# Five-token runs in both halves of the partitions, two load queues, and early attention in a fused linear-attention and GEGLU kernel

## The chip, the cores and the metric

One core of one Trainium2 chip. The metric is the device time of one execution, in microseconds (us), median of several; all executions compared below are in the fast state, except one single look whose state is unknown. Before: 351.67 us (351.45 to 353.07, 3 runs).

## The reference

Linear attention (softmax of q over the features, of k over the tokens), then a gated feed-forward layer on all tokens:

```python
# q, k, v: (8, 8, 576, 64) fp32, randn * 0.1
q_s = softmax(q, axis=-1);  k_s = softmax(k, axis=2)
kv  = np.einsum('bhsd,bhse->bhde', k_s, v)
att = np.einsum('bhsd,bhde->bhse', q_s, kv)
x   = att.transpose(0, 2, 1, 3).reshape(4608, 512)
g   = x @ w_gate                       # (512, 1536)
out = (0.5 * g * (1 + erf(g / sqrt(2))) * (x @ w_val)) @ w_out   # (1536, 512)
```

The softmaxes are written out in the reference (with a subtracted maximum and 1e-9 in the divisor). Since q and k are small, every token of a head gives almost the same row, so an output with permuted rows is only 0.24% off; this matters for reading "correct" in the experiments.

## The kernel before

Block b of the loop is the feed-forward of 512 tokens of batch b; the last block takes the 64 remaining tokens of all eight batches. Attention of the next batch rides between the 12 steps of a block, except in blocks 0 and 1, where it follows the output matmuls. The parts that the argument touches:

```python
# load: partition p holds tokens 4p .. 4p+3 of every head; 64 tokens remain
def load_main(src, nm, b, h0, h1):
    ...
    nc.sync.dma_start(
        out=tiles[key][:, h0:h1, :],                        # 128 partitions
        in_=src[b, h0:h1, 0:MAIN, :].rearrange("h (p n) d -> p h (n d)", n=NM))

def load_rem(src, nm, b):
    t = rmp.tile([64, H, D], f32, name=f"{nm}r", tag="rm")
    nc.sync.dma_start(out=t, in_=src[b, :, MAIN:S, :].rearrange("h p d -> p h d"))
...
# kv of a pair of heads: five matmuls, one per token of the partition (v must be there, cast)
for n in range(NM + 1):
    nc.tensor.matmul(pskv[:, j, :], ek_b[b % 2][:, n, hp * P:(hp + 1) * P],
                     v16_b[b % 2][:, n, 2 * hp:2 * hp + 2, 0:VW], ...)
...
# store of two tokens per partition, 512 KB
nc.sync.dma_start(
    out=out[b * S:b * S + MAIN, :].rearrange("(p n) c -> p n c", n=NM)[:, ns - 1:ns + 1, :],
    in_=yo)
...
for b in range(B + 1):
    ...
    for fi in range(NFI):
        hts.append(ffn_fi(xt, fi))          # 8 matmuls, gelu on ScalarE, product on VectorE
        ...                                 # b >= 2: a unit of the next batch's attention
    ...
    ffn_out(b, hts, 0)                      # 12 matmuls each, evacuation, store
    ...                                     # b <= 1: attention of b + 1 between these
```

The softmax here doesn't subtract the row's maximum and nothing guards it: scores larger than these inputs give would overflow.

## Time and profile before

| | before |
|---|---|
| time | 351.67 us, profiled span 351.8 |
| PE busy | 319.6 us (91%) |
| mean granted PE clock | 0.98 |
| mean DMA rate | 135 GB/s of a span whose first 79 us are full |
| first gate matmul of block 0 / block 1 / block 2 | 26.5 / 70.9 / 111.8 us |
| a block with attention / without | 34.46 / 31.1 us |
| from the last matmul to the end | 4.7 us |

PE is the bound from 111.8 us on; only the first three blocks and the tail have idle PE time. The rows of the profile that show it stand in the prediction below. Two columns need a word: "PEclk" is the clock that PE was granted (it was 0.50 from 66.0 to 70.7 us; the first four gate matmuls of block 0, after 26.5 us of which PE was busy for 7.3, take 1.71 us and later ones 0.86), and "DMA" is the mean over 16 DMA engines.

### The profile page before, as it was taken

The page shows a single profiled execution, that of the slowest core. Times are in us where ns is not written, and L with a number is a line of the kernel's source. Part 1 is how long each engine was busy: PE and PEld are TensorE (multiplying, and loading weights), DVE is VectorE, ACT ScalarE, POOL GpSimd, SP SyncE. Part 2 cuts the span into 40 slices and gives each one's busy share as a digit, 9 for nine tenths or more (in the row PEclk, how much of TensorE's full clock was granted, in tenths as well). Part 3 has the DMA queues.
Part 4 walks back from the last instruction along what each step waited for, and adds up shares of the span by engine and source line. Part 5 has one row for each costly group of instructions (what it writes and reads, how often), then busy time and mean ns, then how long its engine had stood idle before and what let it go on. Part 6 is the DMA issues. An engine that isn't in the chain of part 4 may idle for free.

```text
span 351.8 us, 4287 instructions
## 1 busy us (share of the span) xinstructions
PE 319.6 (91%) x1680; PEld 152.8 (43%) x1680; DVE 179.9 (51%) x283; ACT 135.7 (39%) x184; POOL 42.4 (12%) x36
## 2 busy tenths in 40 slices
PE   0259999499987999999999999999999999999994
PEld 0234445244443544454444444544544444444441
DVE  2582337934386963396339524953494334334331
ACT  3403363043762247424743483248325123203310
POOL 2376620402000200002000200020000000000000
PEclk9999999789996999999999999999999999999999
DMA  7999999893016900296039404940300020011013
GB/s 192 330 388 386 344 278 284 241 269 94 3 60 188 270 6 2 96 276 153 0 117 287 120 2 135 277 112 0 121 1 0 8 113 0 2 60 60 2 30 89
DMA packets 45395, 47.45 MB, mean 135 GB/s; under 512 B 13632, under 2 KB 38208, under 8 KB 45376
## 3 DMA queue, kind: packets, MB, share of 16 engines
q1 hardware_dynamic: 45376, 47.19, 46.3%
q8 instruction: 13, 0.21, 0.3%
q14 instruction: 6, 0.05, 0.1%
HBM read 37.75 MB, written 9.44 MB: 134 GB/s over the span
## 4 chain that ended last, share of the span: by engine, by line
PE 85%; DVE 10%; DMA 2%; issue 1%; SPq 1%; ACT 0%
PE psg L244 27%; PE psv L248 27%; PE psy L262 24%; DVE eq L169 3%; DVE rq L159 2%; PE psx L226 2%; DMA qt<-in_q_dram 2%; PE pst L205 2%; PE pskv L180 2%; DVE xt L229 1%; DVE yo L267 1%; DVE eqt L208 1%; DVE kv_sb L188 1%; PE pstr L214 1%; DVE rrq L163 0%
## 5 line engine op out<-in xcount | busy, mean ns | idle before, releaser
L253 DVE SCALAR_TENSOR_TENSOR ht<-psv,gl 128x512 f16<-128x512 f32 x108 | 74.1, 686 | 92.1 <-PE psv L248 91.5
L251 ACT ACTIVATE gl<-psg 128x512 f32<-128x512 f32 x108 | 64.5, 597 | 144.7 <-PE psg L244 136.1
L244 PE MATMUL psg<-xt,wg_sb 128*128 128x512 f16 x384 | 101.8, 389 | 0.0
L248 PE MATMUL psv<-xt,wv_sb 128*128 128x512 f16 x384 | 99.5, 382 | 0.0
L262 PE MATMUL psy<-wo_sb,ht 128*128 128x512 f16 x432 | 95.0, 379 | 0.0
L248 PEld LDWEIGHTS <-wv_sb 128*128 128x128 f16 x432 | 42.6, 99 | 52.5 <-issue 2.7
L262 PEld LDWEIGHTS <-ht 128*128 128x128 f16 x432 | 41.8, 98 | 49.4
L244 PEld LDWEIGHTS <-wg_sb 128*128 128x128 f16 x432 | 41.6, 99 | 46.0 <-issue 2.8
L267 DVE TENSOR_SCALAR yo<-psy 128x512 f32<-128x512 f32 x36 | 24.8, 690 | 60.7 <-PE psy L262 60.7
L147 POOL CAST v<-vt 128x2048 f16<-128x2048 f32 (+1 forms) x9 | 16.4, 1824 | 179.7 <-DMA vt<-in_v_dram 166.6
L159 DVE TENSOR_REDUCE rq<-eq 128x20 f32<-128x1280 f16 x16 | 23.6, 1476 | 9.6 <-ACT eq L136 9.6
L169 DVE TENSOR_TENSOR eq<-eq,rrq 128x1280 f16<-128x1280 f16 x16 | 25.4, 1590 | 0.2
L205 PE MATMUL pst<-ident,eq 128*128 128x128 f16 x128 | 11.5, 242 | 14.5 <-DVE rck L185 7.8
L180 PE MATMUL pskv<-v,ek 128*128 128x130 f16 x160 | 12.6, 231 | 9.9 <-POOL v L147 9.5
L129 ACT ACTIVATE eq<-qt 128x2048 f16<-128x2048 f32 (+1 forms) x9 | 15.4, 1709 | 6.4 <-DMA qt<-in_q_dram 6.4
L205 PEld LDWEIGHTS <-eq 128*128 128x128 f16 x128 | 9.0, 108 | 19.3 <-DVE eq L169 9.3
L180 PEld LDWEIGHTS <-ek 128*128 128x128 f16 x160 | 11.1, 102 | 13.7 <-ACT ek L129 6.0
L129 ACT ACTIVATE ek<-kt 128x2048 f16<-128x2048 f32 (+1 forms) x9 | 15.5, 1719 | 3.6 <-DMA kt<-in_k_dram 3.5
L238 ACT CAST xtr<-psxr 128x256 f16<-128x256 f32 x8 | 3.0, 372 | 34.9 <-PE psxr L236 34.9
L226 PE MATMUL psx<-eqt,kv_sb 128*128 128x512 f16 x32 | 14.0, 463 | 1.9 <-DVE eqt L208 1.1
L231 ACT CAST xt<-psx 128x512 f16<-128x512 f32 x20 | 11.7, 585 | 9.6 <-PE psx L226 9.6
L248 PE MATMUL psv<-xtr,wv_sb 128*128 128x512 f16 x48 | 12.3, 379 | 0.0
(33 smaller groups left out, 121.1 us busy)
## 6 DMA issues: line engine op xcount, KB each, us to landing
out_dram<-yo SPq DMA_DIRECT2D x16, 512.0 KB, 2.6
kt<-in_k_dram SPq DMA_DIRECT2D x7, 1024.0 KB, 7.9
vt<-in_v_dram SPq DMA_DIRECT2D x7, 1024.0 KB, 10.3
qt<-in_q_dram SPq DMA_DIRECT2D x7, 1024.0 KB, 10.3
wgst<-in_moe_w_gate_dram SPq DMA_DIRECT2D x3, 1024.0 KB, 12.3
wvst<-in_moe_w_val_dram SPq DMA_DIRECT2D x3, 1024.0 KB, 13.6
wost<-in_moe_w_out_dram SPq DMA_DIRECT2D x3, 1024.0 KB, 14.6
kt<-in_k_dram SPq DMA_DIRECT2D x2, 512.0 KB, 5.9
```

The costliest lines, as they stand in the source:

```text
L129: nc.scalar.activation(out=dst[:, 0:NM, h0 * D:h1 * D].rearrange("p n (h d) -> p h n d", d=D), in_=tiles[(nm, b)][:, h0:h1, :].rearrange(" ...
L159: nc.vector.reduce_sum(rq, eq_b[b % 2][:, :, h0 * D:h1 * D].rearrange("p n (h d) -> p n h d", d=D), axis=mybir.AxisListType.X)
L169: nc.vector.tensor_tensor(out=e, in0=e, in1=rr[(b, h0)].unsqueeze(-1).to_broadcast((P, NM + 1, n, D)), op=ALU.mult)
L180: nc.tensor.matmul(pskv[:, j, :], ek_b[b % 2][:, n, hp * P:(hp + 1) * P], v16_b[b % 2][:, n, 2 * hp:2 * hp + 2, 0:VW], start=(n == 0), sto ...
L205: nc.tensor.transpose(pst[:, j, n * P:(n + 1) * P], eq_b[b % 2][:, n, hp * P:(hp + 1) * P], ident)
L226: nc.tensor.matmul(psx, st[(b, "kv", hp)].rearrange("p h e -> p (h e)"), st[(b, "eqt")][:, hp, 0:MAIN], start=True, stop=True)
L244: nc.tensor.matmul(psg, wg_sb[:, ci, fi * P:(fi + 1) * P], xt[:, ci, :], start=(ci == 0), stop=(ci == HP - 1))
L248: nc.tensor.matmul(psv, wv_sb[:, ci, fi * P:(fi + 1) * P], xt[:, ci, :], start=(ci == 0), stop=(ci == HP - 1))
L251: nc.scalar.activation(out=gl, in_=psg, func=ACTF.Gelu)
L253: nc.vector.scalar_tensor_tensor(out=ht, in0=psv, scalar=_H_SCALE, in1=gl, op0=ALU.mult, op1=ALU.mult)
L262: nc.tensor.matmul(psy, hts[fi][:, ns * P:(ns + 1) * P], wo_sb[:, fi, :], start=(fi == 0), stop=(fi == NFI - 1))
L267: nc.vector.tensor_scalar(out=yo[:, ns % 2, :], in0=psy, scalar1=1.0 / _H_SCALE, scalar2=None, op0=ALU.mult)
```

## The change

Its intent is to start PE earlier and close its gaps in blocks 0 and 1. A group of nine tokens now belongs to a pair of partitions m and 64 + m; each of the two loads a run of five (the middle token twice), so the small "remainder" transfers go. Each load and the store pattern are therefore built from two halves of 64 partitions. The start orders q, k, v on two queues, weights come in 1 KB pieces, PE is warmed with idle matmuls, batches 1 and 2 get their attention inside blocks 0 and 1, the last two blocks change places, and the last evacuation (the copy of PE's finished results before a store) is split over two engines.

```diff
-        nc.sync.dma_start(
-            out=tiles[key][:, h0:h1, :],
-            in_=src[b, h0:h1, 0:MAIN, :].rearrange("h (p n) d -> p h (n d)", n=NM))
 ...
+        for t in range(2):
+            engs[t].dma_start(
+                out=tiles[key][64 * t:64 * t + 64, h0:h1, n0 * D:NC * D],
+                in_=src[b, h0:h1].rearrange("h (m n) d -> m h (n d)", n=NT)[
+                    :, :, (4 * t + n0) * D:(4 * t + NC) * D])
 ...
-                nc.sync.dma_start(
-                    out=out[b * S:b * S + MAIN, :].rearrange(
-                        "(p n) c -> p n c", n=NM)[:, ns - 1:ns + 1, :],
-                    in_=yo)
 ...
+        rows = out[b * S:(b + 1) * S, :].rearrange("(m n) c -> m n c", n=NT)
+        def dst(n0, n1, c0=0, c1=C):
+            base = rows[:, 1 + n0:1 + n1, c0:c1]
+            (pm, nm), (pn, _), (pc, nc_) = base.ap
+            return bass.AP(tensor=base.tensor, offset=base.offset,
+                           ap=[[NM * pn, 2], [pm, nm]]
+                           + ([[pn, n1 - n0]] if nc_ != C else [])
+                           + [[pc, nc_ if nc_ != C else (n1 - n0) * C]])
 ...
+    QA = (nc.sync, nc.scalar)
+    load(q, "q", 0, 0, 4, 1, QA)
+    load(q, "q", 0, 4, 8, 1, QA)
+    load(k, "k", 0, 0, H, 0, QA)
+    load(v, "v", 0, 0, H, 0, QA)
+    for c in range(NW):
+        load_w_gv(c)
 ...                                    # all later loads: both halves on nc.sync
+    at(0, NS, 5, L(unit_t, 1, 0))
+    at(0, NS, 6, L(unit_kv, 1, 0))
 ...                                    # attention of batches 1 and 2 in blocks 0 and 1
+            for ns in range(4):        # block 0: output in two halves
+                psys.append(ps_big.tile([P, C], f32, name="psy", tag="mm"))
+                mm_out(psys[ns], hts, ns, range(0, NFI // 2))
+            for ns in range(4):
+                mm_out(psys[ns], hts, ns, range(NFI // 2, NFI))
+                evac(b, ns, psys[ns])
```

(Cut to its core: normalisation by pairs of heads, warming, casts on three engines and the schedule of riders are left out, and the last loop loses its rider calls.)

## The prediction

> **What bounds the kernel now.** I read the page first: PE is busy 91% of 351.8 us, so the end can only move where PE stands still, or runs slowly, or works more. Its second part says where.
>
> ```profile
> PE   0259999499987999999999999999999999999994
> PEclk9999999789996999999999999999999999999999
> DMA  7999999893016900296039404940300020011013
> GB/s 192 330 388 386 344 278 284 241 269 94 3 60 188 270 6 2 96 276 153 0 117 287 120 2 135 277 112 0 121 1 0 8 113 0 2 60 60 2 30 89
> ```
>
> One slice is 8.8 us. PE stands in the first three slices, in slice 8 (62 to 70 us) and in slices 12 and 13; from slice 14 on it is full. The transfers are full for the first 79 us and mostly idle later. Next, the chain of waits in order of time gives the block borders (first gate matmul of each block), and I asked for the busy times between them (columns: PE, weight load, VectorE, ScalarE, GpSimd, clock, DMA share, GB/s).
>
> ```profile
> 0.00:26.50 26.50, 7.26 (x48) 4.78 (x49) 13.49 (x26) 6.66 (x7) 12.58 (x16) 1.00 0.98 303
> 26.50:49.80 23.30, 23.30 (x101) 10.06 (x99) 7.97 (x12) 9.03 (x15) 11.59 (x8) 1.00 1.08 346
> 49.80:70.90 21.10, 16.14 (x97) 8.25 (x96) 16.60 (x24) 5.93 (x5) 6.02 (x4) 0.87 1.00 264
> 92.40:111.80 19.40, 16.14 (x97) 8.25 (x96) 14.89 (x24) 10.46 (x9) 0.00 (x0) 0.86 0.25 79
> 147.08:181.54 34.46, 34.46 (x193) 16.76 (x192) 19.39 (x31) 17.19 (x23) 2.45 (x2) 1.00 0.49 134
> 316.00:347.10 31.10, 31.07 (x144) 13.87 (x142) 11.06 (x16) 7.16 (x12) 0.00 (x0) 1.00 0.14 39
> 347.10:351.80 4.70, 0.00 (x0) 0.00 (x0) 0.69 (x1) 0.00 (x0) 0.00 (x0) 1.00 0.34 78
> ```
>
> A block without attention is 31.1 us (12 steps of 8 matmuls, 1.727 us each, and 48 output matmuls in 10.4); one that carries the next batch's attention is 34.46, so attention costs PE 3.38 us. Against that, block 0 lasts 44.4 (26.5 to 70.9) and block 1 40.9 (to 111.8), because the next attention runs at their ends. The timeline shows one such end: VectorE's normalisation holds the transposes.
>
> ```profile
> 62.72 3.20 DVE L169 TENSOR_TENSOR eq<-eq,rrq 128x1280 f16<-128x1280 f16 x1
> 64.52 1.87 POOL L152 CAST v<-vr 64x512 f16<-64x512 f32 x1
> 65.97 1.04 PE L205 MATMUL pst<-ident,eq 128*128 128x128 f16 x8 [4.22 <-DVE eq L169]
> ```
>
> [...]the first four gate matmuls at 26.69 take 1.71 us against 0.86 later, and full speed comes at 31.6; the clock is 0.50 from 66.0 to 70.7. [...]block 8 stores from 64 partitions, the other blocks from 128. Rows of two DMA views, 336 to 352 us and then 140 to 182 us (40 slices each):
>
> ```profile
> DMA  0000000000000789200589400198800068940000
> GB/s 0 0 0 0 0 0 0 0 0 0 0 0 0 179 195 215 67 0 0 138 179 231 108 0 0 31 210 205 195 16 0 0 148 184 225 97 0 0 0 0
> ```
>
> ```profile
> DMA  0006500079999999999997300000000000008300
> GB/s 0 0 0 277 222 0 0 0 289 217 288 296 245 285 241 292 340 257 252 282 337 182 91 8 0 0 0 0 0 0 0 0 0 0 0 0 351 148 0 0
> ```
>
> Equally busy engines move 195 to 231 GB/s from 64 partitions and 351 from 128. I take 222 GB/s for 64. [...]the trace's 14 loads average 1283.
>
> **The change, part by part.**
>
> *Start.* Both 64-partition halves of q, k, v go out on two queues at once[...]. Before, 1 KB packets reach 347 GB/s around 12.5 us, weights 388 with 2 KB packets. The first landing fits 3.3 us + bytes/rate (k: 0.52 MB, 4.9 us). So q (1.05 MB) lands at 6.3, k (1.31, with the repeated token) at 10.1, v at 13.9 us. Exponentials, normalisation and transposes of q (about 1 us each) fit before v. After v: cast on three engines about 1, both kv groups 1.4 with evacuation 0.8, products and copies 1.2, first weight casts 0.6: block 0 starts near 19 us, not 26.5 (7.5 gained). The 22 warming matmuls save up to 2.5 us of cold clock (26.5 to 31.6 at half rate), if the wait for v lets the clock stay.
>
> *Block 0.* Weight pieces become 1 KB packets: 6.29 MB at 345 GB/s, done at 32.1; a pair of steps needs 1.05 MB (3.0 us) per 3.45 us of PE, so this feeds it. Steps end at 40; first output half (5.2) at 45. w_out 0 to 2 lands at 36.2. From here both halves of a load follow each other on one queue: at 222 GB/s q1 takes 5.9 us (42.1), w_out 3 to 5 comes at 46.1, k1 and v1 by heads at 52.0 and 57.9. At 345 GB/s the last would be 51.6. The second output half waits 2 to 3 us for the last w_out cast, then kv of batch 1 for v. Block 1's first three steps are split so that PE fills the wait; after v lands, cast, kv and the rest put its effective start at v + 1.4 = 59.3, against 70.9: 11.6 gained. Without waits it would be 19 + 34.5 = 53.5, so 5.8 goes to waiting for data.
>
> *Block 1.* 31.1 + attention of batch 2 3.4 + remainder of batch 1 0.5 + about 1 of ScalarE holding the gates (two exponentials between gelus, each 2.3 with two table loads of 1.28, against a reserve of three steps of PSUM, 5.2 us): 36, ends at 95.3.
>
> *Block 2.* 34.46 + remainder of batch 0 (0.5) + stall s: kv of batch 3 stands after its first step, at 97.0, and needs v3 cast. Loads of batch 2 end at 76.2 (0.6 for the small q piece, 3 x 5.9), then block 0's two stores, then batch 3 (17.7).
>
> *Rest.* Four normal normalisations per batch instead of two large ones (a reduction and a product of 1280 columns are 1476 and 1590 ns; halves keep a fixed part) add about 0.7 us to a VectorE that is 56% busy: off the path. Blocks 3 to 6: 4 x 34.46 = 137.8. Blocks 8 and 7: 62.2.
>
> *Stores.* The new store pattern has 2 as its slowest dimension in DRAM (two halves of partitions).[...]
> - 16 engines: stores 2 x 1.5, v3 at 96.9, cast 99.4, s = 2.4. PE ends at 95.3 + 35 + 2.4 + 137.8 + 62.2 = 332.7; tail: half evacuations about 0.8, landing 2.3, end 0.7 = 3.8. **336.5**.
> - 2 engines: a 4 KB packet of an ordinary store has a median of 160 ns in the trace's packet records (2 KB: 84 at best), so 64 packets per engine are 10.2 us. Block 0's pair takes 20.5, v3 lands at 107.7 (those engines' 192 packets take 11), cast 110.2, s = 13.2; PE ends at 343.5. The last block's four stores of 256 KB take 5.3 each, the first starts 6 us before PE's end: 15.3 behind it, and landing 2: tail 17.5. **361**. With fuller load rates s falls to 3 and this becomes 349.
>
> **The rivals.**
> 1. *Two-engine stores* as above.[...] Against: no measurement here, and the change halves its last evacuation over two queues, which is odd beside a tail of 17 us. I give it 0.42.
> 2. *Loads on one queue are no slower*[...]: block 1 starts near 55 and s = 0, giving 330. Against: the halves of block 8's stores follow each other likewise and stay at or below 231.
> 3. *Only the start gains*, because transfers are already 98 to 108% busy up to 70 us and 11% more q, k, v bytes are asked: then block 1 starts at 65, total 342 on 16 engines. Against it: before, weights, batches 0 and 1 (16.5 MB) were there by about 54 us and the end of block 0 was then bound by VectorE, which the change moves under matmuls.
> 4. *Cold PE* in the waits at 13 to 16 and 52 to 59 us: 1 to 3 us in any of these.
>
> **Range and chances.** Sixteen engines: 330 to 342, centre 336.5, nearly all of it below 344.6 (2%). Two: 348 to 366; some 0.4 of it within 2%, 0.5 slower. With 0.58 and 0.42: faster 0.58, same 0.20, slower 0.22. The median of this mixture is 340, toward the upper end of the first part; 329 to 361 holds about 8 in 10.
>
> **What would show it.** First gate matmul near 19 us; w_out's last cast near 48; the first full gate group of block 1 near 60; PE waiting for the GpSimd cast of v after block 2's first step; time from a store's issue to landing 2.6 us (16 engines) or over 10 (2 engines), and from the last matmul to the end 4 or 17 us. It is wrong if block 0 starts after 23 us, if blocks 3 to 6 leave 34.5 us, or if PE's longest waits lie elsewhere than with batches 1 and 3 and the tail.

(That a slowest dimension of 2 might mean two engines stands as assumption, and so does that two queues at once load at the full rate, some 347 GB/s. "The trace's 14 loads" are ScalarE's table loads, 1283 ns each. That halves "keep a fixed part" the kernel after shows: over 640 columns its reduction takes 807 ns and its product 932, where half of the times for 1280 columns would be 738 and 795.)

## The result, and the profile after

After: 390.52 us (388.96 to 391.31, 4 runs) against 351.92 us (351.45 to 353.07, 4 runs) of the kernel before in the same rounds, ratio 1.1086 (1.104 to 1.1133): slower by 11%.

The page's second part, kernel after (40 slices of 9.7 us), and the chain that ended last:

```profile
PE   6499937698962999999959999998799999999910
PEclk9579978899995899999989999999899999999975
DMA  8999999965981796179417942793110010310011
GB/s 170 325 349 358 221 236 205 206 131 144 185 146 49 169 189 117 45 172 208 87 52 170 212 88 81 172 206 63 55 44 2 23 53 34 77 31 3 17 51 41
```

```profile
PE 45%; DMA 33%; SPq 10%; POOL 2%; ACT 2%; issue 2%; DVE 1%; POOLq 0%; ACTq 0%; DVEq 0%
DMA vt<-in_v_dram 21%; PE psg L256 16%; PE psv L256 15%; PE psy L300 11%; SPq L100 8%; DMA wvst<-in_moe_w_val_dram 5%; DMA wost<-in_moe_w_out_dram 5%; POOL v L117 2%; DMA qt<-in_q_dram 2%; PE pskv L182 2%; SPq L111 2%; PE pst L207 1%; PE ps
```

The same chain by engine, kernel before:

```profile
PE 85%; DVE 10%; DMA 2%; issue 1%; SPq 1%; ACT 0%
```

Before, PE carried 85% of the chain that ended last and transfers 2%. Now transfers carry 33%, the load of v alone 21%, and the queue that issues them (SPq) another 10%. PE has new holes in slices 6 to 8, 13, 21 and 28 to 29, and the last two slices are nearly empty. In slice 13 (117 to 127 us) the transfers move 49 GB/s while PE waits: neither of them is full.

The same by blocks (columns as in the prediction: stretch, length, then busy time of PE, weight load, VectorE, ScalarE, GpSimd, then clock, DMA share, GB/s), kernel after; here the start, block 0's output with the gap before block 1, blocks 2, 3 and 4, and the tail:

```profile
0.00:23.25 23.25, 14.49 (x63) 7.01 (x64) 10.57 (x27) 9.11 (x12) 8.52 (x19) 0.71 0.97 264
...
44.30:71.67 27.37, 15.10 (x77) 6.80 (x76) 12.16 (x22) 8.94 (x9) 6.98 (x9) 0.87 1.12 225
...
111.45:159.61 48.16, 37.45 (x202) 18.23 (x200) 22.92 (x41) 23.19 (x26) 4.75 (x3) 0.86 0.56 120
159.61:194.18 34.57, 34.49 (x194) 16.92 (x192) 20.26 (x37) 16.20 (x21) 0.74 (x2) 1.00 0.67 140
194.18:234.72 40.54, 36.17 (x194) 17.27 (x192) 21.75 (x37) 17.80 (x22) 3.29 (x3) 0.96 0.58 127
...
371.55:389.50 17.95, 0.00 (x1) 0.00 (x0) 0.42 (x1) 0.38 (x1) 0.00 (x0) 0.60 0.12 46
```

Block 0 starts at 23.25 us, 3.25 us earlier than before; block 1 at 71.67, no earlier than before. Block 2 takes 48.16 us, blocks 4 and 6 take 40, blocks 3 and 5 the expected 34.5 to 35. Between the last matmul and the end lie 17.95 us.

What PE waits for in block 2 (timeline of PE, kernel after: start, duration, instruction, and in brackets the idle time before it with what ended it):

```profile
112.21 1.03 PE L256 MATMUL psv<-xt,wv_sb 128*128 128x512 f16 x4
123.94 1.24 PE L182 MATMUL pskv<-v,ek 128*128 128x130 f16 x10 [10.71 <-POOL v L117]
124.98 1.91 PE L256 MATMUL psg<-xt,wg_sb 128*128 128x512 f16 x4
126.69 1.91 PE L256 MATMUL psv<-xt,wv_sb 128*128 128x512 f16 x4
```

PE did one step of block 2, then stood 10.7 us for the cast of v of batch 3, and ran its next steps at half clock (0.50 from 123 to 129 us; 1.91 us for four matmuls, 1.03 before). The cast itself waits for the load. Why is the load late? The queue that issues the transfers, kernel after (start and duration of the issuing instructions):

```profile
72.91 3.43 SPq L340 DMA_DIRECT2D out_dram<-yo  x2
76.43 18.46 SPq L100 DMA_DIRECT2D qt<-in_q_dram  x2
95.00 6.47 SPq L100 DMA_DIRECT2D kt<-in_k_dram  x2
101.56 4.94 SPq L100 DMA_DIRECT2D vt<-in_v_dram  x2
```

The two stores of block 0 go out at 72.9, and the two halves of the next q behind them need 18.5 us to be issued, where pairs of load issues that no store precedes take 2.0 to 6.5 in this trace. Something ahead in that queue does not drain. The tail shows the stores alone, from 350 to 390 us (40 slices, kernel after):

```profile
DMA  0000000000000000111111111111111111111100
GB/s 0 16 0 0 0 0 0 8 0 0 0 0 0 0 0 12 33 20 43 49 53 49 53 49 53 49 49 49 49 52 49 51 49 50 51 48 48 41 4 0
```

A share of one tenth and 49 to 53 GB/s: two of sixteen engines. The packet records agree: the 2 KB packets of these last stores have a median of 84 ns, which is 24.4 GB/s for one engine and 49 for two; the 4 KB packets of the earlier stores have 159 ns, 25.8 and 51.5. The records do not name the engine, but they let the engines be counted. The kernel before leaves 1,345 packets of 4 bytes for 84 transfers, 16 for each and one over. The change leaves 1,335 for 100 transfers where e1 below, which differs in the order of its stores alone, leaves 1,601: 266 fewer, 14 for each of 19 stores. (The pages show the same difference: 1846 and 2112 packets under 512 B.) So each of these stores ran on 2 engines and not on 16. The slowest dimension of their destination is 2; whether the number of engines follows it is what e1, e5 and e7 test.

### The profile page after: what moved, and what is told of

It reads as the page before. It is cut to its first block, busy times and chain, and to the rows that moved or that the text cites. A ratio compares the mean times of both kernels' runs of the same rounds, so it can differ in the third digit from the quotient of the medians.

```text
span 389.5 us, 4446 instructions
## 1 busy us (share of the span) xinstructions
PE 329.4 (85%) x1702; PEld 156.6 (40%) x1702; DVE 184.3 (47%) x329; ACT 143.9 (37%) x186; POOL 44.8 (12%) x50
## 2 busy tenths in 40 slices
DMA packets 37068, 50.49 MB, mean 130 GB/s; under 512 B 1846, under 2 KB 32822, under 8 KB 37046
## 4 chain that ended last, share of the span: by engine, by line
PE 45%; DMA 33%; SPq 10%; POOL 2%; ACT 2%; issue 2%; DVE 1%; POOLq 0%; ACTq 0%; DVEq 0%
DMA vt<-in_v_dram 21%; PE psg L256 16%; PE psv L256 15%; PE psy L300 11%; SPq L100 8%; DMA wvst<-in_moe_w_val_dram 5%; DMA wost<-in_moe_w_out_dram 5%; POOL v L117 2%; DMA qt<-in_q_dram 2%; PE pskv L182 2%; SPq L111 2%; PE pst L207 1%; PE psx L234 1%; ACT gl L261 1%; DVE ht L263 0%
## 5 line engine op out<-in xcount | busy, mean ns | idle before, releaser
L300 PE MATMUL psy<-wo_sb,ht 128*128 128x512 f16 x432 | 98.0, 384 | 6.4 <-POOL wo_sb L117 4.3
L256 PE MATMUL psv<-xt,wv_sb 128*128 128x512 f16 x384 | 102.6, 388 | 0.0
L335 DVE TENSOR_SCALAR yo<-psy 128x512 f32<-128x512 f32 x31 | 21.3, 689 | 50.0 <-PE psy L300 50.0
L117 POOL CAST v<-vt 128x2048 f16<-128x2048 f32 (+5 forms) x18 | 20.7, 1178 | 199.2 <-DMA vt<-in_v_dram 199.2
L182 PE MATMUL pskv<-v,ek 128*128 128x130 f16 x160 | 13.7, 243 | 24.8 <-POOL v L117 20.1
L156 DVE TENSOR_REDUCE rq<-eq 128x10 f32<-128x640 f16 (+1 forms) x32 | 25.3, 792 | 8.3 <-ACT eq L139 8.3
L139 ACT ACTIVATE ek<-kt 128x2560 f16<-128x2560 f32 (+1 forms) x10 | 19.0, 1908 | 24.7 <-DMA kt<-in_k_dram 24.7
L159 DVE TENSOR_TENSOR eq<-eq,rrq 128x640 f16<-128x640 f16 (+1 forms) x28 | 25.6, 915 | 1.0
L119 ACT CAST xt<-psx 128x512 f16<-128x512 f32 x24 | 14.0, 585 | 18.4 <-PE psx L234 18.4
L139 ACT ACTIVATE eq<-qt 128x2560 f16<-128x2560 f32 (+1 forms) x9 | 18.5, 2053 | 5.0 <-DMA qt<-in_q_dram 4.9
L139 ACT ACT_TABLE_LOAD x8 | 10.3, 1283 | 16.1 <-DMA qt<-in_q_dram 16.0
L256 PE MATMUL psg<-xtr,wg_sb 128*128 128x512 f16 x48 | 12.3, 379 | 0.0
```

Of the source, the lines that this page charges most:

```text
L117: nc.gpsimd.tensor_copy(out=dst, in_=src)
L139: nc.scalar.activation(out=dst[:, n0:NC, h0 * D:h1 * D].rearrange("p n (h d) -> p h n d", d=D), in_=tiles[(nm, b)][:, h0:h1, n0 * D:NC * D ...
L156: nc.vector.reduce_sum(rq, e, axis=mybir.AxisListType.X)
L159: (nc.gpsimd if eng == "pool" else nc.vector).tensor_tensor(out=e, in0=e, in1=rrq.unsqueeze(-1).to_broadcast((P, n, 2, D)), op=ALU.mult)
L256: nc.tensor.matmul(ps, w[:, ci, fi * P:(fi + 1) * P], xt[:, ci, :], start=(ci == 0), stop=(ci == HP - 1))
L300: nc.tensor.matmul(psy, hts[fi][:, ns * P:(ns + 1) * P], wo_sb[:, fi, :], start=(fi == 0), stop=(fi == NFI - 1))
```

## The experiments

Two defects are now suspected: stores on two engines, and loads into 64 adjacent partitions. The expectations set two theories against each other: 1, the stores hold up the loads behind them; 2, the loads are too slow by themselves and the stores matter at the end alone. A third suspect is the new schedule itself. That the late v needs both defects was not foreseen; it came out of the runs. The first four kernels take each defect away alone and both together, on one chip in the same rounds (before: 352.26 us, 7 runs).

### e1_swap: stores on 16 engines, wrong row order on purpose

```diff
-                           ap=[[NM * pn, 2], [pm, nm]]
+                           ap=[[pm, nm], [NM * pn, 2]]
```

The two dimensions in DRAM change places, so that the slowest is 64. Rows then land in the wrong order; the output still passes the tolerance (0.24% off), so "correct" says nothing here.

> The changed kernel with one edit: in each main store the two outer dimensions of the DRAM pattern are swapped, so that the slowest one is 64 and not 2. Same rows, bytes and packets; the rows within a block come out in another order, so the result is wrong on purpose. Theory 1 (stores run on 2 engines, and hold up the loads behind them): time from a store's issue to landing falls from over 10 us to about 2.6, the tail from 17.9 to about 4 us, and the waits for v in blocks 2, 4, 5 and 6 (13.3, 6.0, 0.5 and 5.2 us over an undisturbed block) go: 389.5 - 13.9 - 25 = 351. Theory 2 (stores are no matter except at the end; loads into 64 partitions are too slow by themselves): only the tail goes, 376, and the waits stay.

Measured: 353.57 us (352.0 to 354.04), ratio 1.0023 (0.9989 to 1.0057), the same as before. Against the change this is 37 us less: the tail falls from 17.95 to 4.2 us, and the waits inside the blocks go, since PE never waits for the GpSimd cast of v in this run. But block 1 still starts late (70.3 us, 71.7 in the change).

### e2_swap_last: the same only in the last block

```diff
-                           ap=[[NM * pn, 2], [pm, nm]]
+                           ap=([[pm, nm], [NM * pn, 2]] if b == order[-1] else [[NM * pn, 2], [pm, nm]])
```

The rows of the last block are wrong.

> The same swap in the last block's stores alone (wrong row order in that block on purpose). Both theories: only the tail changes, 17.9 to about 4 us, so 375 to 377. Should it be nearer 351, the stores before the last block would matter little to the waits and theory 1 would have the wrong place.

Measured: 376.6 us (374.23 to 377.54), ratio 1.0662 (1.0617 to 1.0707). So 13.9 us (390.5 - 376.6) of the 37 are the tail alone, and the other 23 lie inside the blocks. PE's waits for the cast of v stay: 20.5 us in all, against 20.1 in the change.

### e3_load128: loads over 128 partitions, stores as in the change

```diff
-        for t in range(2):
+        hm = (h0 + h1) // 2
+        for t, (ha, hb) in enumerate(((h0, hm), (hm, h1))):
+            base = src[b, ha:hb, n0:MAIN + n0, :].rearrange("h (p n) d -> p h (n d)", n=NM)
+            (pp, _), (ph, _), (pd, _) = base.ap
             engs[t].dma_start(
-                out=tiles[key][64 * t:64 * t + 64, h0:h1, n0 * D:NC * D],
-                in_=src[b, h0:h1].rearrange("h (m n) d -> m h (n d)", n=NT)[
-                    :, :, (4 * t + n0) * D:(4 * t + NC) * D])
+                out=tiles[key][:, ha:hb, n0 * D:NC * D],
+                in_=bass.AP(tensor=base.tensor, offset=base.offset,
+                            ap=[[pp, P], [ph, hb - ha], [pd, (NC - n0) * D]]))
```

Same number of transfers, same bytes, same 1280-byte packets; each transfer now covers all partitions and half of the heads. The tokens are wrong (runs of five that start four apart).

> The changed kernel with its stores as they are, but each pair of loads into 64 partitions replaced by two loads of half the heads into all 128 (runs of five tokens that start four tokens apart; same bytes and packet size; other tokens, so wrong on purpose). If 64 partitions halve a load's rate: GB/s between 36 and 70 us rises from 200 to 240 to about 330, block 0 starts some 3 us and block 1 some 8 us sooner. Theory 1: the tail stays at 17.9 us and there are still waits for v, since two engines stay behind: 370 to 382. Theory 2: waits for v go too and 355 to 360 is left.

Measured: 349.05 us (348.76 to 351.15), ratio 0.9915 (0.9879 to 0.9952). Neither theory's number holds (370 to 382, 355 to 360): with the slow stores still there it is 41 us less than the change. The tail stays (17.5 us), but the longest wait of PE for the GpSimd cast of v is 2.1 us in place of 10.7.

### e4_swap_load128: both

Both edits above; wrong.

> Both edits (wrong on purpose): what the schedule of the change gives without either defect of its transfers. If nothing else is wrong with it: start near 20, block 1 near 63, no waits for v, tail about 4: 334 to 340, so faster than before by 3 to 5%. If it stays above 345, a third cause is in the schedule itself.

Measured: 334.76 us (334.48 to 334.86), ratio 0.9496 (0.9474 to 0.9518).

The four together, medians in us:

| | loads of 64 adjacent partitions | loads of 128 partitions | load fix saves |
|---|---|---|---|
| stores on 2 engines | 390.5 (the change) | 349.1 (e3) | 41.4 |
| stores on 16 engines | 353.6 (e1) | 334.8 (e4) | 18.8 |
| store fix saves | 36.9 | 14.3 | |

(The change's own number is from an earlier set of rounds, in which the kernel before had 351.92.) If the defects only added up, both columns would save the same. They do not: some 23 us appear only when both are there. The load rates show the load defect alone. Windows of 12 us at 36 to 48 and 60 to 72 us, first the kernel after, then e4 (columns as above):

```profile
36.00:48.00 12.00, 12.00 (x58) 5.42 (x56) 4.09 (x6) 4.27 (x6) 4.16 (x4) 1.00 1.10 248
...
60.00:72.00 12.00, 6.14 (x44) 3.28 (x43) 5.84 (x12) 4.75 (x7) 3.43 (x5) 0.93 1.14 203
```

```profile
36.00:48.00 12.00, 11.25 (x55) 5.01 (x53) 6.31 (x10) 6.08 (x5) 4.22 (x5) 1.00 1.06 371
...
60.00:72.00 12.00, 11.39 (x65) 5.45 (x64) 8.10 (x14) 9.42 (x12) 2.45 (x2) 1.00 1.06 378
```

The engines are just as busy (1.06 to 1.14) and move 203 GB/s in one and 378 in the other. (In e4, block 0's stores pass among them; from 66 to 72 us, with almost only loads in both, it is 204 and 363.) The median time of a 1280-byte packet after 150 us is 108 ns in the change, 112 in e1, and 55 in e3 and e4. So the busy share did not tell slow transfers from fast ones; the rate and the packet time did.

How both defects together make v late can be worked out for the two engines that carry stores; it is not seen directly, since the records do not name engines. (That successive stores share the same two fits the tail, where four of them, issued from 364.5 us on, together stay at 49 to 53 GB/s.) In one block each of them has 2 x 64 store packets of 159 ns, 20.4 us, and 192 load packets. With 128-partition loads those take about 192 x 55 ns = 10.6 us: 31 us, which fits in a block of 34.5, and e3 shows nearly no wait. In the change the GpSimd casts of v of batches 3 to 7, which wait for the loads, start at 120.85 and then up to 271.85 us, 37.75 us apart on average; less 20.4 leaves 17.4 us for 192 load packets, some 90 ns each (an estimate, if those two engines are always busy). That is more than PE's 34.5 us for a block, so on this account two engines set the period, while the mean share is 0.58 to 0.67 and everything else waits for them.

### e5_before_store2 and e7_before_store4: the store defect alone, in the kernel before

```diff
+                base = out[b * S:b * S + MAIN, :].rearrange(
+                    "(p n) c -> p n c", n=NM)[:, ns - 1:ns + 1, :]
+                (pp, _), _, (pc, _) = base.ap
                 nc.sync.dma_start(
-                    out=out[b * S:b * S + MAIN, :].rearrange(
-                        "(p n) c -> p n c", n=NM)[:, ns - 1:ns + 1, :],
-                    in_=yo)
+                    out=bass.AP(tensor=base.tensor, offset=base.offset,
+                                ap=[[pp, 2], [2 * pp, P // 2], [pc, 2 * C]]),
+                    in_=yo.rearrange("p n c -> p (n c)"))
```

e7 has `[[pp, 4], [4 * pp, P // 4], ...]` instead: a slowest dimension of 4. Rows are wrong in both. These and the next two ran on another chip, with before at 351.91 us (7 runs). They ask whether the number of engines really follows the slowest dimension, and whether the slow store costs anything by itself.

> The kernel before with one thing of the change: its main stores get a DRAM pattern whose slowest dimension is 2 (2 x 64 rows, another row order, wrong on purpose; same rows, bytes, packets). Theory 1 (the slowest dimension sets the number of engines): a store lands some 12 us after its issue instead of 2.6, moves near 50 GB/s, and its loads, with 2 engines behind, come late. The kernel before prefetches as far ahead and moves 10% less, from 128 partitions at full rate, so there is more slack than in the change: 352 to 362. The tail stays near 4.7 us plus what block 7's two stores leave behind (block 8's stores are unchanged). If the rule is wrong: 352 and 2.6 us to landing.

> The same with a slowest dimension of 4 (4 x 32 rows). Theory 1: 4 engines, about 100 GB/s, landing some 6.5 us after issue, time within 1% of before. If only the pattern's irregular order mattered and not its slowest dimension, it would look like the run with 2.

The transfers from 300 us to the end (40 slices), first e5, then e7; the last block's stores, after the gap, are unchanged in both:

```profile
DMA  1000000001111111111111111100000253526260
GB/s 55 29 13 0 0 0 0 0 0 26 32 39 45 51 51 58 51 51 51 51 58 51 51 64 51 51 0 0 0 0 0 69 137 71 135 67 138 55 151 0
```

```profile
DMA  0000000000122222222210000000000043535353
GB/s 0 0 0 13 0 0 0 0 0 0 28 66 38 54 82 101 101 101 101 85 50 0 0 0 13 0 0 0 0 0 0 0 110 91 121 80 121 80 123 79
```

51 GB/s with 2 and 101 GB/s with 4, beside 351 GB/s for the ordinary store of the kernel before: 25 GB/s per engine; in these runs the number of engines was the slowest dimension where that was 2 or 4. The small packets count the engines again: against the kernel before, e5 has 224 fewer (14 for each of its 16 changed stores) and e7 192 fewer (12 for each). Yet e5 took 352.87 us (352.34 to 353.68), ratio 1.0024 (0.9985 to 1.0063): the same as before. Its stores crawl, but its loads are fast, its last block stores with 64 as slowest dimension, and nobody waits for the others: PE waits for the GpSimd cast of v once, for 9.3 us, as in the kernel before (9.5). The queue is held all the same. Behind block 0's stores, the small load of k at 66.11 us in e5 takes 16.64 us to be issued (0.97 in the kernel before), and the two halves of q at 58.97 us in e3 take 15.73. So the held queue, 18.5 us in the change, comes with the two-engine stores whatever the loads are, and does not by itself make v late: where the loads are fast, v is still there in time, or almost.

e7 was looked at once, 354.69 us, state unknown; its time decides nothing, only its rate is used.

### e6_interleave: a correct version with both defects removed

Run t of group m moves from partition 64t + m to 2m + t. A load of one t then steps over every second partition, and the store's DRAM pattern gets 64 as its slowest dimension and is right. The middle token that is held twice is now masked by a 0/1 column per partition instead of by half of the partitions.

```diff
-                out=tiles[key][64 * t:64 * t + 64, h0:h1, n0 * D:NC * D],
+                out=tiles[key][t:P:2, h0:h1, n0 * D:NC * D],
 ...
-                           ap=[[NM * pn, 2], [pm, nm]]
+                           ap=[[pm, nm], [NM * pn, 2]]
 ...
-            copy_on(eng, d[0:64, 0, h0:h1, 0:D], t[0:64, h0:h1, 0:D])
+            dst, src0 = d[:, 0, h0:h1, 0:D], t[:, h0:h1, 0:D]
+            if eng == "act":
+                nc.scalar.activation(out=dst, in_=src0, func=ACTF.Copy, scale=even)
+            else:
+                (nc.gpsimd if eng == "pool" else nc.vector).tensor_scalar(
+                    out=dst, in0=src0, scalar1=even, scalar2=None, op0=ALU.mult)
 ...
-        nc.vector.tensor_copy(out=st[(b, "eqtr")], in_=pst[:, :, 0:REM])
+        nc.vector.tensor_copy(out=st[(b, "eqtr")],
+                              in_=pst[:, :, 0:REM] if b == 0 else pst[:, :, 0:P:2])
```

> A right version of the change without either defect: token run t of group m goes to partition 2m + t instead of 64t + m. Each load of 64 partitions then steps by two[...]; each store has 64 as its slowest dimension. The second copy of the doubled token is zeroed by a mask per partition[...]. Theories 1 and 2 together: like the run with both edits, 333 to 340 us, faster than before by 3 to 5.5%.[...]

(The other case: loads still at 200 to 240 GB/s, and 350 to 354 us.)

Measured: 336.53 us (336.17 to 337.0), ratio 0.9559 (0.9529 to 0.9588), correct. Because the check on the chip cannot see permuted rows, its arithmetic was also recomputed on the host: 0.06% from the reference, as the change is. It beats the kernel before by 4.4% and the change by about 14% (336.5 against 390.5, on another chip). The page, kernel e6:

```profile
PE   7599997998999999999999999999999999999995
...
DMA  7999999991149003930294019601100110041002
GB/s 227 359 348 357 376 364 312 383 363 37 63 151 354 32 2 128 357 113 0 101 338 158 3 63 324 211 0 65 63 0 2 63 63 2 0 94 31 3 31 95
```

In slice 9 (67 to 75 us), after the weights and block 0's stores, loads of 64 partitions alone reach 363 GB/s, where those of 64 adjacent ones moved 204 in the change (66 to 72 us): with the same number of partitions, which ones they were made the difference. And at the start, where the halves run on two queues at once, the same stretch (4 to 6 us) reads as follows in the kernel after and then in e6:

```profile
4.00:6.00 2.00, 2.00 (x6) 0.65 (x5) 0.00 (x0) 1.60 (x3) 0.00 (x0) 1.00 1.15 214
```

```profile
4.00:6.00 2.00, 2.00 (x6) 0.63 (x5) 0.00 (x0) 1.90 (x3) 0.00 (x0) 1.00 1.14 353
```

In this stretch two queues with one half each move 214 GB/s in the change, not 353. But a little later, when k and v pass, one half on each queue, they move 357 in the same trace:

```profile
12.00:14.00 2.00, 2.00 (x9) 0.82 (x6) 1.46 (x4) 0.26 (x1) 0.92 (x1) 0.50 1.07 357
```

From 10 to 14 us the two queues finish 557 and 556 of the load packets, with a median of 60 ns. So adjacent halves on two queues are at times slow and at times not, and these runs do not settle on what it depends. In e6 block 0 starts at 19.46 us, in e4 at 17.9. The waits of PE for the cast of v, first the kernel after, then e6 (total, number, longest, us):

```profile
PE pskv L182 <- POOL v L117: 20.1, 5, 10.7
```

```profile
PE pskv L193 <- POOL v L160: 0.8, 1, 0.8
```

### e8_interleave_nowarm: e6 without the 22 warming matmuls

```diff
-    warm_pe(16)
 ...
-    warm_pe(6)
```

> The same without the 22 warming matmuls. If they keep the clock up into block 0 they are worth up to 2.5 us (5.1 us at half rate in the kernel before); if the wait for v lets it fall anyway, under 1 us.

Measured: 337.3 us (336.24 to 337.33), ratio 0.9572 (0.9541 to 0.9603), beside 0.9559 of e6: no difference that these runs can show. Block 0 starts at 20.47 us without the warming and at 19.46 with it, and in both the four matmuls before it run cold (1.91 us). (PEclk reads 1.00 at that time in e8; at the start of a trace the length of four matmuls tells more.) With the warming PE still stands for 2.3 us before the first kv matmuls, which wait for v; without it 3.6.

## Why the prediction was wrong

The predicted number lies between two branches; the one with stores on two engines, 361 us, is the one that holds. It got a weight of 0.42, and it was itself 28.5 us short of the profiled span of 389.5. Three steps failed: the choice between the branches, the rate and order of the loads, and the pace of blocks 3 to 6. One by one:

**The choice between the branches.** "No measurement here", the prediction said against two engines, "and the change halves its last evacuation over two queues, which is odd beside a tail of 17 us". The first is no evidence either way, and the second is a guess about intent. The grounds for two engines no run of the kernel before shows, so the weights of 0.58 and 0.42 were the author's estimate. The tail (17.95 us, predicted 17.5), the stall of block 2 (48.16 us, predicted 35 + 13.2 = 48.2) and the last two blocks (62.16, predicted 62.2) came out as that branch worked them out; e2 confirms the tail as a cause by itself. For block 2 this is in part luck: PE stood 10.7 us, not 13.2, and 2.6 us of half clock, which that sum left out, made up the rest.

**The terms that were too small in that branch**, in us:

| step as predicted | predicted | measured | miss |
|---|---|---|---|
| effective start of block 1, "v + 1.4 = 59.3" | 59.3 | 73.8 | 14.5 |
| block 1 | 36 | 37.6 | 1.6 |
| block 2 | 48.2 | 48.16 | 0 |
| "Blocks 3 to 6: 4 x 34.46 = 137.8" | 137.8 | 149.8 | 12.0 |
| blocks 8 and 7, tail | 79.7 | 80.1 | 0.4 |

(73.8 is the end of block 1's first three steps, 79.02, less three normal steps, 5.18.) The sum of the misses is 28.5, and 361 + 28.5 = 389.5, the span.

- *Start.* The step that failed is "Both 64-partition halves of q, k, v go out on two queues at once", which was reckoned at the full rate of some 347 GB/s. From 2 to 10 us they move 201 to 235 GB/s; only from 10 to 14 us is it 357. The casts of v start at 17.96 us, not 13.9, and block 0 starts at 23.25, not 19. With loads at the full rate (353 GB/s from 4 to 6 us in e6) the rest of this step's working is sound: 17.9 us in e4, 19.46 in e6. Why the two stretches differ stays open here.
- *Load rate on one queue.* "At 222 GB/s" was a pick near the top of the 195 to 231 seen in stores; the loads moved some 200 (198 to 209 in stretches between 60 and 72 us). The last w_out cast ended at 57.6 us, not 48. The last half of v of batch 1 landed at 68.7, not 57.9, which is 10.8 of the 14.5. The rate is the smaller part of that. By the packet records, as many bytes as all loads up to this v hold (17.04 MB) had been moved by 62.4 us, 4.5 late, of which 2.0 at the last gate and value weights already (34.1, predicted 32.1). The other 6.3 us pass because loads queued behind it, of batch 2, move before its last packets: the halves did not follow "each other on one queue" in the order in which the prediction let them land. The remaining 3.7 of the 14.5 are the work after it (5.1 in place of 1.4), partly at low clock. With the late start (5.3 us) this is the 18.8 us that e1 loses to e4: from block 2 on the outputs of both follow each other in the same 34.56 or 31.08 us, and each of e1's begins 19.3 us after e4's.
- *Blocks 3 to 6.* The prediction counted the two slow engines' packets once, for batch 3, with "192 packets take 11", 57 ns each, and then let the blocks run at PE's pace. With loads into 64 adjacent partitions they take some 90 ns (an estimate, above), the sum of stores and loads on those engines is 37.75 us and not under 34.5, and v is late again in blocks 4 and 6 (40.54 and 39.66 us). e3 and e1 each take one half of this sum away, and the waits go.

The store fix of e1 can be followed through the profiles in the same way: by the end of block 2 it is 11.9 us ahead of the change, blocks 3 to 8 add 11.6 and the tail 13.8, together 37.3, beside 36.9 in the medians.

**The other branch was mis-sized too.** With 16 engines it said 336.5; e1 measured 353.6, 17 us more, because block 1 is as late there as in the change. That e6 measures 336.5 is chance: it also has the full load rate, for which rival 2 said 330, and e4 measured 334.8. The prediction's aside on two engines did hold: "With fuller load rates s falls to 3 and this becomes 349". That is e3, 349.05 us, with a block 2 of 38.6 us, 3.0 over that of e4.

**The rivals.** Two-engine stores: right. "Loads on one queue are no slower": wrong, by the 363 against 204 GB/s above. "Only the start gains": wrong in sign, since nothing of the 3.25 us that the start gained reached block 1. "Cold PE": real but small; in block 2 PE is busy 37.45 us for what takes 34.83 in e1, 2.6 us. The new schedule itself is not at fault: e4 and e6, which keep all of it, gain 4.4 to 5%. Which of its parts earns this, the start or the attention inside blocks 0 and 1, no run takes apart.

**What I checked it against.** The prediction named its own failing signs, and all of them showed: block 0 after 23 us, blocks 3 to 6 not at 34.5, waits with batches other than 1 and 3.

## What to carry to other kernels

Before a change of layout goes in, read each transfer's pattern twice: in these runs the slowest dimension on the DRAM side decided how many engines worked (2, 4 or 16), and for loads on one queue the set of partitions on the chip how fast (204 GB/s into 64 adjacent ones, 363 into all 128); with a step of two partitions the same split in halves reached 363 too. A mean DMA share of 0.6 beside a PE that waits for data hid here that two engines were behind, and a share of 1.1 that the packets were slow: look at GB/s and the time of one packet, not at the share. And test two suspects alone and together: each by itself cost 14 to 19 us in this schedule, but together they cost 56, and the slow stores cost nothing in the kernel before.
